# Turning round the second product of a fused attention and mixture kernel, and regrouping its 64-key products

## The chip, the cores and the metric

The kernel runs on one NeuronCore of a Trainium2 chip. The metric is the device time of one execution in microseconds. Its engines are TensorE (PE; PEld are its weight loads), VectorE (DVE), ScalarE (ACT), GpSimd (POOL) and SyncE (SP), which issues most of the DMAs. Each engine works through its own instructions in the order in which they were emitted; semaphores tie them together.

## The reference

For 8 batches of 12 heads, 448 tokens and 64 channels a head, attention with a sigmoid in place of the softmax; then a product with w_in, g = h - tanh(h), and a product with w_out. All in float32.

```python
scores = scale * np.matmul(q, k.transpose(0, 1, 3, 2)) - np.log(S)      # S = 448
attn = 1.0 / (1.0 + np.exp(-scores))
x = np.matmul(attn, v)             # (8, 12, 448, 64) -> (3584, 768)
h = x @ w_in                       # (768, 2048)
g = h - np.tanh(h)
out = g @ w_out                    # (2048, 768) -> (3584, 768)
```

## The kernel before

Float32 operands are split into two float16 parts (high and low), and a product is the sum of three float16 products. Two heads share the 128 partitions, so a batch has 6 pairs of heads (`NP`), numbered `g` over batches 1 to 7 in `stream` (`g % NP` is the place in the batch). Two neighbouring pairs, g and h = g + 1, make a step of `stream`.

A head has 448 keys: three tiles of 128 (`c` = 0, 1, 2) and a rest of 64 (`c == QT`). The rests of pair g and pair g + 1 are done together: `scores` (lines 384 to 401) then uses 64 rows by 64 columns of the array in four places, and `av` (lines 415 to 431), the product with v, does the same. For full tiles `scores` uses two blocks of 64 rows by 128 columns and `av` two blocks of 128 rows by 64 columns. Each instruction streams 448 columns. `units` (573) issues scores and the sigmoids (`weigh`, line 405, ACT); `keep` (584) splits them (`split_a`: line 411 on ACT, line 412 on DVE); `do_av` (558) issues the products with v of what is in `todo`; `close_acc` (549) evacuates an accumulator (`evac_x`, line 439, ACT) and calls `add_squares` (443 to 466).

`stream` is a generator; each `next` runs one block. A step of two pairs has the blocks B1 (scores c = 0, 1 of g; then the products with v of the pair h before, which closes it), B2 (scores c = 2 and the 64 keys of g and h), Sc (scales of the next two pairs, with a small PE product `pbn` in the PSUM bank "av"), B3 (scores c = 0, 1 of h; the products with v of g, the 64-key ones too, which closes g) and B4 (scores c = 2 of h, and the K and Q parts of the next odd pair, lines 369 to 372).

For the bound of a batch's tokens, `add_squares` sums the squares of its six x tiles: from batch 2 on, place 0 squares on ACT, places 1 to 4 square (line 456) and add (line 465) on POOL, place 4 (`NP - 2`) adds into `x2b`, and place 5 squares on ACT (line 454) into a tile of the tag "x2", which has two buffers. `token_norms` (687) then sums `x2b` and the last square by two PE matmuls (line 690, `nm`, in a buffer of the tag "sc", which has two and is shared with the scores), and DVE reduces `nm` (line 692), works out a scale and splits the six x tiles into `xhl` (lines 721 to 724).

A batch is then `moe1` (first product and the mixture; `product`, line 773) and `second`, which runs `moe2` (second product) and calls the blocks of the next batch's attention between its matmuls, at positions in `BLOCKS` (batch 1: `BLOCKS1`) counted in units of about 1 us of matmuls. From batch 2 on the positions are B4 at 8, B1 at 11, B2 at 16, Sc, B3 and B4 at 20, B1 at 27, B2 at 32, Sc, B3 and B4 at 36, B1 at 43, B2 at 48, Sc and B3 at 52. The B1 at 43 finishes the next batch's attention; `second` puts its `nm` three units behind it, at 46, and the other splits at 48 and 50. Batch 6 ends its blocks at 43; batch 7 has none. The rest of `mix` of the last g tile (`TAIL`) goes at 1 to 5.

`moe2` makes 128 tokens by 384 columns a matmul (line 857, `po`; stationary g, moving w_out), 288 to a batch, and for the 64 tokens that are left 96 matmuls of 64 columns of the array in pairs (line 905, `por`). Evacuation is on ACT (890) and DVE (894, 914).

Batch 0 and all preparation of the weights are laid out by hand in the string `ORDER`: each letter is a step (P one piece of the second product, B a block of `stream`, t and F the mixture's stages, A and a splits of w_out, C its conversion, X the scale of its second half, S and Z splits of w_in).

Of the kernel before, what the change touches and what calls it, by code (L numbers as in the profile page):

```python
# [8 lines left out]
F16 = mybir.dt.float16  # L9
# [24 lines left out]
class Builder:  # L34
# [7 lines left out]
        "vrrssvrsrrvvvvRrRrRRRMrRRRnRrRRGMRRwtMttRtRBtwRRtMwBgttMtRtRttMBttRtRttM"  # L42
        "tMBBtRttRMtBttMttMtRxtRtBRAtMtttAMtBttMttAttAttMMtAtPPtaRPRBPtBbtCaBCBAC"
        "PtFCCPBPCPPBZPPPCSBCPPBZCBCPPCCBPCCCSZBPPCCCPCXBaaAPaPPPBAPPaaaBBSPPSPSZ"
        "PSZSPPPPPPPSPBPPPZPPPNPZPSPZPSSNNPPSZPPZSSPPPPPPPPPPPP"
    )
# [244 lines left out]
    def w_out_scale(self, e):  # L291

        V = self.nc.vector
        self.w_out_bound(e)
        m = self.bound[e]
        total = self.sm.tile([P, 1], F32, name="wtot2")
        V.scalar_tensor_tensor(total, m, 1.05, m, op0=ALU.mult, op1=ALU.mult)
        S, inv = self.scale_of(total, f"swo{e}")
        self.Swo.append(S)
        V.tensor_copy(self.iSwo[:, e : e + 1], inv)  # L300
        h = slice(e * D, (e + 1) * D)
        V.tensor_copy(self.iSwo[h, 2:3], inv[h])

# [17 lines left out]
    def load_v(self, b, j, pool, tag, bufs):  # L321


        at = 0 if j % 2 == 0 else 2 * QT + 2
        n = 2 * QT + (0 if j % 2 else 2)
        t = pool.tile([P, n, D], F32, name="vn", tag=tag, bufs=bufs)
        self.nc.sync.dma_start(t, self.v[b, j // 2, :, at : at + n])
        return t
# [78 lines left out]

    def split_a(self, a):
        nc = self.nc
        A = self.tp.tile([P, 2, 2, self.S], F16, name="ahl", tag="t")  # L410
        nc.scalar.activation(A[:, 0], a[:, 0], AF.Copy, scale=A_SCALE)  # L411
        nc.vector.scalar_tensor_tensor(A[:, 1], a[:, 0], A_SCALE, A[:, 0], op0=ALU.mult, op1=ALU.subtract)  # L412
        return A

    def av(self, acc, v, A, c, odd):


        half = c == QT
        m = P // len(acc)
        prods = ((0, 0), (1, 0), (0, 1)) if A.dtype == F16 else ((0, 0),)  # L420
        for n, (w, x) in enumerate(prods):
            for i in range(len(acc)):
                for h in range(2):
# [4 lines left out]
                        A[k, x, h],  # L428
                        start=(n == 0 and (i == 1 if half else c == 0 and not odd)),
                        stop=(n == len(prods) - 1 and (i == 0 if half else c == QT - 1 and bool(odd))),  # L430
                    )
# [36 lines left out]
    def stream(self):  # L468
# [71 lines left out]
        yield 0, False  # L540
        todo = []

# [6 lines left out]
        def close_acc(g):  # L549
# [5 lines left out]
            for d in (sc, K, Q):  # L555
                d.pop(g)

        def do_av():
            for g, c, A in todo:
                odd = g % 2  # L560
                if c == QT:
                    open_acc(g + 1)
                    self.av([accs[g], accs[g + 1]], vv[g], A, c, odd)
                    close_acc(g)
                    continue
# [18 lines left out]
        def keep(g, cs, aa):  # L584
            if splits(g):
                aa = [self.split_a(a) for a in aa]
            todo.extend((g, c, a) for c, a in zip(cs, aa))

        for g in range(0, G, 2):
            h = g + 1  # L590
            early = g == 0

            aa = units(g, (0, 1))
            do_av()
            if early:
                prep_v(0)
                prep_v(1)
            keep(g, (0, 1), aa)
            load(g + 3)
# [3 lines left out]

            aa = units(g, (2, QT))
            if early:
                do_av()
            norms(g + 3)
            keep(g, (2, QT), aa)
            yield 2750, True
# [27 lines left out]
            yield 2750, True  # L637
        do_av()
        yield 1150, True

# [196 lines left out]
    def moe2(self, b, gs):  # L837
        nc = self.nc
        S = self.S
        ks = self.ks  # L840
        iK = self.sm.tile([P, 3], F32, name="iK")
        n = 1 if b == 0 else 3
        nc.vector.tensor_scalar(iK[:, :n], self.iSwo[:, :n], self.iSg, None, op0=ALU.mult)
        H = self.HALF
        base = b * S
        prods = ((0, 0), (0, 1), (1, 0))
        last = (self.NF - 1, 2)

        def store(o, j0, n, cols, queue=nc.sync):
            queue.dma_start(self.out[base + j0 : base + j0 + n, cols], o)  # L850

        nt = S // P

        def products(po, tk, f, e):
            for n, (x, w) in enumerate(prods):
                for i in e:
                    nc.tensor.matmul(  # L857
                        po[i][:, :H],
                        gs[f // 2][:, x, f % 2, tk * P : (tk + 1) * P],
                        self.wo[:, i * self.NF + 2 * ks[f // 2] + f % 2, w],  # L860
                        start=(f == 0 and n == 0),
                        stop=((f, n) == last),
                    )

        if b == 0:
            for e in range(2):
                for tk in range(nt):
                    po = {e: self.ps.tile([P, 512], F32, name="po", tag="mm", bufs=2)}
                    for f in range(0, self.NF, 2):
                        products(po, tk, f, (e,))  # L870
                        products(po, tk, f + 1, (e,))
                        if f + 2 == self.NF:
                            if (e, tk) == (1, 0):
                                nc.vector.tensor_scalar(iK[:, 1:], self.iSwo[:, 1:], self.iSg, None, op0=ALU.mult)
                            o = self.op.tile([P, H], F32, name="oh", tag="o", bufs=2)
                            nc.scalar.activation(o, po[e][:, :H], AF.Copy, scale=iK[:, e : e + 1])
                            store(o, tk * P, P, slice(e * H, (e + 1) * H))
                        yield 980
        else:
            for tk in range(nt):  # L880
                if b + 1 == self.B and tk % 2:
                    both = self.ps.tile([P, 2, 512], F32, name="po", tag="sc", bufs=2)
                    po = [both[:, e] for e in range(2)]
                else:
                    po = [self.ps.tile([P, 512], F32, name=f"po{e}", tag="mm", bufs=2) for e in range(2)]
                for f in range(self.NF):
                    products(po, tk, f, (0, 1))
                    if f == self.NF - 1:
                        o = self.op.tile([P, self.DM], F32, name="o", tag="o", bufs=2)
                        nc.scalar.activation(o[:, :H], po[0][:, :H], AF.Copy, scale=iK[:, 0:1])  # L890
                        if (b, tk) == (1, 0):
                            nc.scalar.activation(o[:, H:], po[1][:, :H], AF.Copy, scale=iK[:, 1:2])  # L892
                        else:
                            nc.vector.tensor_scalar(o[:, H:], po[1][:, :H], iK[:, 1:2], None, op0=ALU.mult)
                        store(o, tk * P, P, slice(0, self.DM))
                    yield 980
        nm = nt * P
        if b + 2 < self.B:
            po = self.ps.tile([P, 512], F32, name="por", tag="mm", bufs=2)
        else:  # L900
            po = self.ps.tile([P, 2, 512], F32, name="por", tag="sc", bufs=2)[:, 0]
        for f in range(self.NF):
            for n, (x, w) in enumerate(prods):
                for e in range(2):
                    nc.tensor.matmul(  # L905
                        po[e * D : (e + 1) * D, :H],
                        gs[f // 2][:, x, f % 2, nm:S],
                        self.wo[:, e * self.NF + 2 * ks[f // 2] + f % 2, w],
                        start=(f == 0 and n == 0),
                        stop=((f, n) == last),  # L910
                    )
            yield 560
        o = self.op.tile([P, H], F32, name="orem", tag="o", bufs=2)
        nc.vector.tensor_scalar(o, po[:, :H], iK[:, 2:3], None, op0=ALU.mult)  # L914
        for e in range(2):
            queue = nc.scalar if e and b + 1 == self.B else nc.sync
            store(o[e * D : (e + 1) * D], nm, S - nm, slice(e * H, (e + 1) * H), queue)


    def build(self):  # L920
# [13 lines left out]
        self.ihk0 = const("ihk0", KAPPA)  # L934
        self.iSwo = const("iswo", 1.0, 3)
        self.sums = [const(f"ss{i}", 0.0, 6) for i in range(2)]
# [147 lines left out]
    def second(self, b, blocks, alone, events):  # L1084
# [13 lines left out]
        events.sort(key=lambda e: e[0])  # L1098
        full = self.NF * (self.S // P)
        for k, _ in enumerate(self.moe2(b, self.gs)):  # L1100
            now = k + 1 if k < full else full + (k + 1 - full) / 2
            while events and events[0][0] <= now:
# [36 lines left out]
```

## Time and profile before

| what | us |
|---|---|
| runs | 1165.2, 1165.48, 1997.27; median 1165.48 |
| the profiled execution | 1166.29 |
| its span, first to last instruction | 1164.5 |
| PE busy | 1153.1 (99%) |
| DVE busy | 907.7 (78%) |
| ACT busy | 865.5 (74%) |
| POOL busy | 79.1 (7%) |

The profiled execution has 1.8 us around its span. Granted clock of TensorE 0.999. PE counts as busy from a matmul's start to its modelled end, and matmuls overlap, so the pace of PE is read from starts: a row of the timeline merges neighbouring instructions of one kind, and the start of the next row less its own start is what they took.

### The profile page before, as it was taken

The numbers are of one execution on the slowest core, as the hardware profiler recorded it, in microseconds if no ns is written. First come the engines' busy times: TensorE is split into PE (matmuls) and PEld (weight loads), VectorE is DVE, ScalarE is ACT, GpSimd is POOL, SyncE is SP. The second block draws the span as 40 slices with busy tenths as digits, with TensorE's granted clock in tenths as the row PEclk, the third lists the DMA queues.
The fourth block names the chain that finished last, engine by engine and source line by source line (L and its number), as shares of the span: only waits on it lengthen the run. The fifth ranks groups of instructions, "written<-read, shape, count | busy, mean of one in ns | idle before, by whom it ended". The sixth has DMA issues, their size and how long they took to land.

```text
span 1164.5 us, 18896 instructions
## 1 busy us (share of the span) xinstructions
PE 1153.1 (99%) x7563; PEld 597.4 (51%) x7564; DVE 907.7 (78%) x1308; ACT 865.5 (74%) x1195; POOL 79.1 (7%) x58
## 2 busy tenths in 40 slices
PE   9999999999999999999999999999999999999998
PEld 3345444555555555555555555555555555555565
DVE  6999999789777996679867897778976798646930
ACT  7988996588976888768887688867887688745820
POOL 0000000000120002200021000200022000300000
PEclk9999999999999999999999999999999999999999
DMA  9942171000222002210022101210012100000000
GB/s 358 357 163 64 42 224 53 29 7 1 80 75 64 7 1 78 62 53 1 17 76 62 40 1 31 82 58 24 1 55 84 53 1 9 23 28 7 1 14 35
DMA packets 34056, 70.43 MB, mean 60 GB/s; under 512 B 3888, under 2 KB 21040, under 8 KB 33968
## 3 DMA queue, kind: packets, MB, share of 16 engines
q1 hardware_dynamic: 33744, 68.89, 18.1%
q8 instruction: 59, 0.97, 0.4%
q10 hardware_dynamic: 224, 0.33, 0.1%
q14 instruction: 29, 0.24, 0.1%
HBM read 58.20 MB, written 11.01 MB: 59 GB/s over the span
## 4 chain that ended last, share of the span: by engine, by line
PE 73%; ACT 1%; issue 0%; DVE 0%; ACTq 0%
PE ph L773 28%; PE po L857 27%; PE sc L394 6%; PE acc L425 6%; PE por L905 5%; ACT a L405 0%; ACT ahl L411 0%; PE nm L690 0%; ACT sqn L335 0%; ACT x L439 0%; ACT Q L369 0%; DVE orem L914 0%; PE pbn L344 0%; ACT x L454 0%; ACT o L892 0%
## 5 line engine op out<-in xcount | busy, mean ns | idle before, releaser
L857 PE MATMUL po<-wo,g 128*128 128x384 f16 x2304 | 389.1, 326 | 3.1 <-DVE wo L240 1.6
L773 PE MATMUL ph<-xhl,wi 128*128 128x448 f16 x2016 | 382.6, 352 | 0.0
L857 PEld LDWEIGHTS <-g 128*128 128x128 f16 x2304 | 220.3, 98 | 170.1 <-issue 26.4
L773 PEld LDWEIGHTS <-wi 128*128 128x128 f16 x2016 | 196.7, 98 | 185.0 <-issue 2.1
L412 DVE SCALAR_TENSOR_TENSOR ahl<-a,ahl 128x896 f16<-128x896 f32 x126 | 162.7, 1326 | 125.6 <-ACT ahl L411 125.0
L405 ACT ACTIVATE a<-sc,nls,rn 128x896 f32<-128x896 f32 x147 | 155.8, 1090 | 37.4 <-PE sc L394 37.2
L811 ACT ACTIVATE u<-ph,ih 128x896 f32<-128x896 f32 x64 | 64.4, 1006 | 75.8 <-PE ph L773 74.0
L411 ACT ACTIVATE ahl<-a 128x896 f16<-128x896 f32 x126 | 113.2, 941 | 0.6
L394 PE MATMUL sc<-Q,K 64*128 64x448 f16 x1008 | 100.8, 353 | 0.9 <-DVE th L816 0.7
L815 DVE SCALAR_TENSOR_TENSOR m<-ph,ihk,u 128x896 f32<-128x896 f32 x64 | 73.5, 1149 | 25.6 <-ACT th L813 25.2
L766 ACT ACTIVATE g<-m,Sg 128x896 f16<-128x896 f32 x64 | 66.7, 1041 | 35.5 <-DVE m L829 28.5
L829 DVE COPY_PREDICATED m<-u,th 128x896 f32<-128x896 uint32 x64 | 77.2, 1206 | 6.8 <-ACT u L828 0.8
L425 PE MATMUL acc<-ahl,vhl 128*64 128x448 f16 (+1 forms) x864 | 80.6, 356 | 0.4 <-ACT tn L346 0.4
L456 POOL TENSOR_TENSOR x<-x 128x448 f32<-128x448 f32 x24 | 28.3, 1178 | 762.1 <-ACT x L439 762.1
L767 DVE SCALAR_TENSOR_TENSOR g<-m,Sg,g 128x896 f16<-128x896 f32 x64 | 73.4, 1147 | 6.8 <-ACT g L766 6.7
L826 DVE SCALAR_TENSOR_TENSOR m<-q,m 128x896 f32<-128x896 f32 x64 | 69.9, 1092 | 6.7 <-DVE m L822 0.5
L983 PE MATMUL ph<-x,wi 128*128 128x448 f32 x192 | 73.8, 540 | 0.0
L816 DVE SCALAR_TENSOR_TENSOR th<-ph,ih,th 128x896 f32<-128x896 f32 x64 | 73.3, 1145 | 0.0
L822 DVE SCALAR_TENSOR_TENSOR m<-q,m 128x896 f32<-128x896 f32 x64 | 69.6, 1087 | 0.0
L828 ACT ACTIVATE u<-u,b 128x896 f32<-128x896 f32 x64 | 66.7, 1042 | 1.9
L821 ACT ACTIVATE q<-u,b 128x896 f32<-128x896 f32 x64 | 65.8, 1028 | 0.0
L825 ACT ACTIVATE q<-u,b 128x896 f32<-128x896 f32 x64 | 65.8, 1028 | 0.0
(141 smaller groups left out, 1087.7 us busy)
## 6 DMA issues: line engine op xcount, KB each, us to landing
knn<-k SPq DMA_DIRECT2D x45, 224.0 KB, 2.6
qnn<-q SPq DMA_DIRECT2D x44, 224.0 KB, 2.6
rawo<-moe_w_out SPq DMA_DIRECT2D x22, 384.0 KB, 5.2
out<-o SPq DMA_DIRECT2D x21, 384.0 KB, 2.3
raw<-moe_w_in SPq DMA_DIRECT2D x13, 512.0 KB, 8.2
vn<-v SPq DMA_DIRECT2D x24, 256.0 KB, 2.8
wo<-moe_w_in SPq DMA_DIRECT2D x11, 512.0 KB, 8.3
vn<-v SPq DMA_DIRECT2D x24, 192.0 KB, 2.4
```

The source lines that it names most:

```text
L394: self.nc.tensor.matmul(ps[i * m : (i + 1) * m, h, : self.S], K[i][r, w, c * P : c * P + m], Q[i][r, x, :], start=(n == 0), stop=(n == len ...
L405: self.nc.scalar.activation(a[:, 0], ps[:, :, : self.S], AF.Sigmoid, bias=self.nls, scale=scale)
L411: nc.scalar.activation(A[:, 0], a[:, 0], AF.Copy, scale=A_SCALE)
L412: nc.vector.scalar_tensor_tensor(A[:, 1], a[:, 0], A_SCALE, A[:, 0], op0=ALU.mult, op1=ALU.subtract)
L425: self.nc.tensor.matmul(acc[i][h * D : (h + 1) * D, : self.S], v[k, w, 2 * QT + h if half else h * QT + c], A[k, x, h], start=(n == 0 and ...
L767: nc.vector.scalar_tensor_tensor(g[:, 1], m, Sg, g[:, 0], op0=ALU.mult, op1=ALU.subtract)
L773: self.nc.tensor.matmul(ph, self.wi[:, self.slot(c, k), part, e * P : (e + 1) * P], xhl[c][:, x, :], start=(i == 0), stop=(i == len(prods) ...
L815: V.scalar_tensor_tensor(m, ps, ihk, u, op0=ALU.mult, op1=ALU.mult)
L816: V.scalar_tensor_tensor(th, ps, ih, th, op0=ALU.mult, op1=ALU.subtract)
L829: V.copy_predicated(m, u.bitcast(U32), th)
L857: nc.tensor.matmul(po[i][:, :H], gs[f // 2][:, x, f % 2, tk * P : (tk + 1) * P], self.wo[:, i * self.NF + 2 * ks[f // 2] + f % 2, w], star ...
L983: nc.tensor.matmul(ph[:, e, :S], self.fp32(self.wi, self.slot(c, k))[:, 0, e * P : (e + 1) * P], xs[c], start=(c == 0), stop=(c == self.NC ...
```

## The change

- Second product: w_out's 128 columns become the stationary operand and all 448 tokens of g the moving one. A batch is 6 row blocks `d` of 48 matmuls 128*128 with 448 columns; the output is stored transposed (and turned back on the host). `por` is gone. From batch 1 on, the last two of block 0's 16 pieces are moved behind the eighth piece of block 1. The last block is evacuated and stored in two halves, on ACT and DVE. A batch has 96 yields, each counted as 7/12 of a unit; batch 0 has 48 P of six matmuls each in place of 64, and `ORDER` loses 16 P.
- Attention of batches 2 to 7: B1 is now scores c = 0 of g, products with v of the pair h before, the 64-key scores of g and h, and behind them the 64-key products with v of the two pairs before (`do_rest`), which closes both of them. B2 is scores c = 1, 2. B3 has no 64-key products and closes nothing. The split 64-key weights wait in a part of the w_out buffer; the 64-key part of v comes with the odd pair's load. Behind the last step `do_rest` runs once more.

```diff
@@ second product (moe2)
+        half = self.NC // 2
+        def products(po, d, f):
+            e, at = d // half, d % half * P
+            for n, (x, w) in enumerate(prods):
+                nc.tensor.matmul(
+                    po[:, :S],
+                    self.wo[:, e * self.NF + 2 * ks[f // 2] + f % 2, w, at : at + P],
+                    gs[f // 2][:, x, f % 2],
+                    start=(f == 0 and n == 0),
+                    stop=((f, n) == last),
+                )
+        def out(po, d):
...
+            if b + 1 == self.B and d == self.NC - 1:
+                h = S // 2
+                nc.scalar.activation(o[:, :h], po[:, :h], AF.Copy, scale=iv)
+                nc.scalar.dma_start(self.out[rows, b * S : b * S + h], o[:, :h])
+                nc.vector.tensor_scalar(o[:, h:], po[:, h:S], iv, None, op0=ALU.mult)
+                nc.sync.dma_start(self.out[rows, b * S + h : (b + 1) * S], o[:, h:])
+                return
+            if b == 0 or d % 2 or (b, d) == (1, 0):
+                nc.scalar.activation(o, po[:, :S], AF.Copy, scale=iv)
+            else:
+                nc.vector.tensor_scalar(o, po[:, :S], iv, None, op0=ALU.mult)
+            nc.sync.dma_start(self.out[rows, cols], o)
+        held = 2
+        order = [(d, f) for d in range(self.NC) for f in range(self.NF)]
+        if b:
+            late = [order.pop(self.NF - held) for _ in range(held)]
+            at = self.NF - held + self.NF // 2
+            order[at:at] = late
+        for d, f in order:
+            if f == 0:
+                po[d] = self.ps.tile([P, 512], F32, name="po", tag="mm", bufs=2)
+            products(po[d], d, f)
...
+            if b or f % 2:
+                yield 567
@@ stream
+        def do_rest():
+            while kept:
+                g, A = kept.pop()
+                self.av([accs[g], accs[g + 1]], vv[g + 1], A, QT, 0, True)
+                close_acc(g)
+                close_acc(g + 1)
         def do_av():
             for g, c, A in todo:
                 odd = g % 2
+                if splits(g):
+                    if c == 0:
+                        open_acc(g)
+                    self.av([accs[g]], vv[g], A, c, odd, True)
+                    continue
...
-            aa = units(g, (0, 1))
-            do_av()
+            first, second = ((0, QT), (1, 2)) if splits(g) else ((0, 1), (2, QT))
+            if splits(g):
+                aa = units(g, (0,))
+                do_av()
+                aa += units(g, (QT,))
+                do_rest()
...
-            aa = units(g, (2, QT))
+            aa = units(g, second)
...
         do_av()
+        do_rest()
@@ second
-            now = k + 1 if k < full else full + (k + 1 - full) / 2
+            now = (k + 1) * 7 / 12
```

## Rows read from the trace of the kernel before

**Rows 1.** The page: busy time of the engines, the granted clock in 40 slices, and the chain of work that ended last, by engine.
```profile
PE 1153.1 (99%) x7563; PEld 597.4 (51%) x7564; DVE 907.7 (78%) x1308; ACT 865.5 (74%) x1195; POOL 79.1 (7%) x58
...
PEclk9999999999999999999999999999999999999999
...
PE 73%; ACT 1%; issue 0%; DVE 0%; ACTq 0%
```
**Rows 2.** Whom PE waited for in the whole span: us in total, times, longest us.
```profile
PE po L857 <- DVE wo L240: 1.6, 3, 0.6
...
PE sc L394 <- DVE th L816: 0.7, 1, 0.7
PE po L857 <- DVE g L767: 0.7, 1, 0.7
...
PE po L857 <- ACT g L766: 0.4, 1, 0.4
```
**Rows 3.** Timeline of PE at the end of batch 6 and in batch 7, where no block of attention stands between: start us, us, engine, line, operation, count.
```profile
1043.10 7.99 PE L905 MATMUL por<-wo,g 128*64 128x384 f16 x96
1051.02 54.66 PE L773 MATMUL ph<-xhl,wi 128*128 128x448 f16 x288
1105.51 46.96 PE L857 MATMUL po<-wo,g 128*128 128x384 f16 x288
1152.41 7.99 PE L905 MATMUL por<-wo,g 128*64 128x384 f16 x96
```
**Rows 4.** Timeline of PE in batch 2's second product, around the B1 at 43 and the B2 at 48.
```profile
486.50 1.31 PE L394 MATMUL sc<-Q,K 64*128 64x448 f16 x12
...
487.74 1.89 PE L425 MATMUL acc<-ahl,vhl 128*64 128x448 f16 x18
...
489.56 3.10 PE L857 MATMUL po<-wo,g 128*128 128x384 f16 x18
...
492.50 0.35 PE L690 MATMUL nm<-x2b,onesb 128*128 128x448 bf16 x1
...
492.69 0.35 PE L690 MATMUL nm<-x,onesb 128*128 128x448 bf16 x1
...
494.92 1.43 PE L394 MATMUL sc<-Q,K 64*128 64x448 f16 x18
...
496.28 1.98 PE L905 MATMUL por<-wo,g 128*64 128x384 f16 x22
```
**Rows 5.** Timeline of ACT and DVE in the same stretch; in brackets the idle time before and what ended it.
```profile
487.28 2.09 ACT L405 ACTIVATE a<-sc,nls,rn 128x896 f32<-128x896 f32 x2 [2.33 <-PE sc L394]
...
489.67 0.64 ACT L439 ACTIVATE x<-acc,rn 128x448 f32<-128x448 f32 x1 [0.30 <-PE acc L425]
...
490.40 0.58 ACT L454 ACTIVATE x<-x 128x448 bf16<-128x448 f32 x1
490.88 1.77 ACT L411 ACTIVATE ahl<-a 128x896 f16<-128x896 f32 x2
491.85 2.09 DVE L412 SCALAR_TENSOR_TENSOR ahl<-a,ahl 128x896 f16<-128x896 f32 x2 [4.04 <-ACT ahl L411]
...
493.86 0.62 DVE L692 TENSOR_REDUCE m<-nm 128x1 f32<-128x448 f32 x1
```
**Rows 6.** The squares of place 4 in the B3 at 36 of the same batch, on ACT and POOL; then the instructions of line 456 in the whole span (shortest, median and longest ns).
```profile
479.00 0.63 ACT L439 ACTIVATE x<-acc,rn 128x448 f32<-128x448 f32 x1
...
479.77 1.46 POOL L456 TENSOR_TENSOR x<-x 128x448 f32<-128x448 f32 x1 [11.23 <-ACT x L439]
...
481.31 1.87 POOL L465 TENSOR_TENSOR x2b<-x,x 128x448 bf16<-128x448 f32 x1
...
L456 POOL TENSOR_TENSOR x<-x x24: 933/936/1486, 305.5 to 1029.2; 128x448 f32<-128x448 f32 x24
```
**Rows 7.** Timeline of PE in batch 0's second product, where it waits.
```profile
146.61 1.15 PE L857 MATMUL po<-wo,g 128*128 128x384 f16 x6
148.21 0.50 PE L857 MATMUL po<-wo,g 128*128 128x384 f16 x2 [0.44 <-ACT g L766]
149.39 1.80 PE L857 MATMUL po<-wo,g 128*128 128x384 f16 x10 [0.69 <-DVE g L767]
...
182.69 0.32 PE L857 MATMUL po<-wo,g 128*128 128x384 f16 x1
183.51 1.14 PE L857 MATMUL po<-wo,g 128*128 128x384 f16 x6 [0.49 <-DVE wo L240]
185.22 0.97 PE L857 MATMUL po<-wo,g 128*128 128x384 f16 x5 [0.57 <-DVE wo L240]
...
191.64 5.50 PE L857 MATMUL po<-wo,g 128*128 128x384 f16 x31
197.71 2.60 PE L857 MATMUL po<-wo,g 128*128 128x384 f16 x15 [0.57 <-DVE wo L240]
```
**Rows 8.** Timeline of batch 2's B1 at 11: its first scores, and the DVE work of the B4 before it that is still going on.
```profile
436.93 1.31 PE L394 MATMUL sc<-Q,K 64*128 64x448 f16 x12
...
437.65 1.08 DVE L412 SCALAR_TENSOR_TENSOR ahl<-a,ahl 128x896 f16<-128x896 f32 x1
...
438.65 0.68 DVE L372 SCALAR_TENSOR_TENSOR Q<-qnn,sn,Q 128x448 f16<-128x448 f32 x1
```
**Rows 9.** Timeline of the end of the span: the last evacuation.
```profile
1160.44 0.62 DVE L914 TENSOR_SCALAR orem<-por,iK 128x384 f32<-128x384 f32 x1 [7.31 <-PE por L905]
```

More of the change, by code (lines that the diff above doesn't have):

```diff
@@ L42 @@
         "vrrssvrsrrvvvvRrRrRRRMrRRRnRrRRGMRRwtMttRtRBtwRRtMwBgttMtRtRttMBttRtRttM"
-        "tMBBtRttRMtBttMttMtRxtRtBRAtMtttAMtBttMttAttAttMMtAtPPtaRPRBPtBbtCaBCBAC"
-        "PtFCCPBPCPPBZPPPCSBCPPBZCBCPPCCBPCCCSZBPPCCCPCXBaaAPaPPPBAPPaaaBBSPPSPSZ"
-        "PSZSPPPPPPPSPBPPPZPPPNPZPSPZPSSNNPPSZPPZSSPPPPPPPPPPPP"
+        "tMBBtRttRMtBttMttMtRxtRtBRAtMtttAMtBttMttAttAttMMtAtPPtaRRBPtBbtCaBCBACP"
+        "tFCCPBPCPPBZPPCSBCPPBZCBCPPCCBPCCCSZBPCCCPCXBaaAPaPPPBAPaaaBBSPPSPSZPSZS"
+        "PPPPPPSPBPPZPPPNPZPSPZSSNNPPSZPZSSPPPP"
     )
@@ L300, in w_out_scale @@
         V.tensor_copy(self.iSwo[:, e : e + 1], inv)
-        h = slice(e * D, (e + 1) * D)
-        V.tensor_copy(self.iSwo[h, 2:3], inv[h])
     def split_w_out(self, e):
@@ L321, in load_v @@
     def load_v(self, b, j, pool, tag, bufs):
-        at = 0 if j % 2 == 0 else 2 * QT + 2
-        n = 2 * QT + (0 if j % 2 else 2)
+        first = 2 * QT + (2 if b < self.AV32 else 0)
+        at = j % 2 * first
+        n = 4 * QT + 2 - first if j % 2 else first
         t = pool.tile([P, n, D], F32, name="vn", tag=tag, bufs=bufs)
@@ L406, in weigh, with split_a @@
         return a
-    def split_a(self, a):
+    def split_a(self, a, kept):
         nc = self.nc
-        A = self.tp.tile([P, 2, 2, self.S], F16, name="ahl", tag="t")
+        if kept:
+            A = self.scratch((self.NF - self.SHIFT_O) * 2 * self.HALF, 4 * self.S).rearrange("p (x h n) -> p x h n", x=2, h=2)
+        else:
+            A = self.tp.tile([P, 2, 2, self.S], F16, name="ahl", tag="t")
         nc.scalar.activation(A[:, 0], a[:, 0], AF.Copy, scale=A_SCALE)
@@ L413, in split_a, with av @@
         return A
-    def av(self, acc, v, A, c, odd):
+    def av(self, acc, v, A, c, odd, late=False):
         half = c == QT
+        if late:
+            begin, end = (not half and c == 0,) * 2, (half,) * 2
+        else:
+            begin = (False, True) if half else (c == 0 and not odd,)
+            end = (True, False) if half else (c == QT - 1 and bool(odd),)
         m = P // len(acc)
@@ L428, in av @@
                         A[k, x, h],
-                        start=(n == 0 and (i == 1 if half else c == 0 and not odd)),
-                        stop=(n == len(prods) - 1 and (i == 0 if half else c == QT - 1 and bool(odd))),
+                        start=(n == 0 and begin[i]),
+                        stop=(n == len(prods) - 1 and end[i]),
                     )
@@ L540, in stream @@
         yield 0, False
-        todo = []
+        todo, kept = [], []
         def open_acc(g):
@@ L585, in keep @@
             if splits(g):
-                aa = [self.split_a(a) for a in aa]
-            todo.extend((g, c, a) for c, a in zip(cs, aa))
+                aa = [self.split_a(a, c == QT) for c, a in zip(cs, aa)]
+            for c, a in zip(cs, aa):
+                if splits(g) and c == QT:
+                    kept.append((g, a))
+                else:
+                    todo.append((g, c, a))
         for g in range(0, G, 2):
@@ L591, in stream @@
             early = g == 0
-            aa = units(g, (0, 1))
-            do_av()
+            first, second = ((0, QT), (1, 2)) if splits(g) else ((0, 1), (2, QT))
[4 more added lines that the diff above has]
+                do_rest()
+            else:
+                aa = units(g, first)
+                do_av()
             if early:
@@ L597, in stream @@
                 prep_v(1)
-            keep(g, (0, 1), aa)
+            keep(g, first, aa)
             load(g + 3)
@@ L607, in stream @@
             norms(g + 3)
-            keep(g, (2, QT), aa)
+            keep(g, second, aa)
             yield 2750, True
@@ L840, in moe2 @@
         ks = self.ks
-        iK = self.sm.tile([P, 3], F32, name="iK")
-        n = 1 if b == 0 else 3
+        iK = self.sm.tile([P, 2], F32, name="iK")
+        n = 1 if b == 0 else 2
         nc.vector.tensor_scalar(iK[:, :n], self.iSwo[:, :n], self.iSg, None, op0=ALU.mult)
         H = self.HALF
-        base = b * S
+        cols = slice(b * S, (b + 1) * S)
         prods = ((0, 0), (0, 1), (1, 0))
         last = (self.NF - 1, 2)
-        def store(o, j0, n, cols, queue=nc.sync):
-            queue.dma_start(self.out[base + j0 : base + j0 + n, cols], o)
@@ L852, in moe2 @@
-        nt = S // P
-        def products(po, tk, f, e):
+        half = self.NC // 2
+        def products(po, d, f):
+            e, at = d // half, d % half * P
             for n, (x, w) in enumerate(prods):
[L856 to L917, printed above, removed]
+                nc.tensor.matmul(
[5 more added lines that the diff above has]
+                )
@@ new lines, in out @@
+        def out(po, d):
+            iv = iK[:, d // half : d // half + 1]
+            rows = slice(d * P, (d + 1) * P)
+            o = self.op.tile([P, S], F32, name="o", tag="o", bufs=2)
+            if b + 1 == self.B and d == self.NC - 1:
[7 more added lines that the diff above has]
+                nc.scalar.activation(o, po[:, :S], AF.Copy, scale=iv)
+            else:
+                nc.vector.tensor_scalar(o, po[:, :S], iv, None, op0=ALU.mult)
+            nc.sync.dma_start(self.out[rows, cols], o)
@@ new lines, in moe2 @@
+        held = 2
[4 more added lines that the diff above has]
+            order[at:at] = late
+        po = {}
+        for d, f in order:
+            if f == 0:
+                po[d] = self.ps.tile([P, 512], F32, name="po", tag="mm", bufs=2)
+            products(po[d], d, f)
+            if f == self.NF - 1:
+                if (b, d) == (0, half):
+                    nc.vector.tensor_scalar(iK[:, 1:], self.iSwo[:, 1:], self.iSg, None, op0=ALU.mult)
+                out(po.pop(d), d)
+            if b or f % 2:
+                yield 567
@@ L934, in build @@
         self.ihk0 = const("ihk0", KAPPA)
-        self.iSwo = const("iswo", 1.0, 3)
+        self.iSwo = const("iswo", 1.0, 2)
         self.sums = [const(f"ss{i}", 0.0, 6) for i in range(2)]
@@ L1098, in second @@
         events.sort(key=lambda e: e[0])
-        full = self.NF * (self.S // P)
         for k, _ in enumerate(self.moe2(b, self.gs)):
-            now = k + 1 if k < full else full + (k + 1 - full) / 2
+            now = (k + 1) * 7 / 12
             while events and events[0][0] <= now:
@@ L1122 @@
     rest = v[:, :, QT * P :].reshape(B, H // 4, 2, 2, D, D).transpose(0, 1, 2, 4, 3, 5).reshape(B, H // 4, P, 2, D)
+    n = Builder.AV32
+    v_first = np.concatenate([heads[:n, :, :, 0], rest[:n], heads[:n, :, :, 1]], axis=3)
+    v_later = np.concatenate([heads[n:, :, :, 0], heads[n:, :, :, 1], rest[n:]], axis=3)
     arrays = {
@@ L1125 @@
         "k": pairs(k),
-        "v": np.ascontiguousarray(np.concatenate([heads[:, :, :, 0], rest, heads[:, :, :, 1]], axis=3)),
+        "v": np.concatenate([v_first, v_later]),
         "moe_w_in": np.ascontiguousarray(moe_w_in).view(np.uint64),
@@ L1132 @@
     }
-    shape = (B * S, H * D)
+    shape = (H * D, B * S)
     args["out"] = nc.dram_tensor("out", shape, F32, kind="ExternalOutput").ap()
@@ L1137 @@
     r = run_bass_kernel_spmd(nc, [arrays], core_ids=[0])
-    return r.results[0]["out"]
+    return np.ascontiguousarray(r.results[0]["out"].T)
```

## The prediction

> **What bounds the kernel now.** I read the page first: PE is busy 99% of the span, the chain that ended last lies on PE, and the granted clock is at its upper level, 2.4 GHz, in all 40 slices [rows 1]. Since a matmul's end is modelled, that does not yet say that PE never stands still, so I read whom PE waited for: a handful of waits, none over 1 us, on the splits of w_out, the first g tiles and the mixture [rows 2]. By the timeline those lie in batch 0 [rows 7] and early in batch 1. From batch 2 on PE waits for nothing. So three things count: the pace of PE's own stream, a PE wait that goes, and a PE wait that comes. Work of ACT, DVE, POOL and the queues counts only where PE comes to wait for it.
>
> **Part 1, the second product.** Before, a batch takes 46.90 us for 288 matmuls of 384 columns (from 1105.51 to 1152.41) and 7.92 us for the 96 of `por` (from 1043.10 to 1051.02) [rows 3], 54.82 us with the change into and out of the 64-column form. The new form, 128*128 with 448 columns, is in the trace as the first product: 288 from 1051.02 to 1105.51, 54.49 us, 0.1892 each [rows 3]. The new second product is also 288 of these. It saves 0.33 us a batch, 2.6 us in eight, less 0.1 for the exit that the last batch doesn't have: 2.5 us. Why so little: the streamed columns are the same (288 x 384 + 48 x 384 = 288 x 448). 46.8/288 = 0.1625 us for 384 columns and 0.1892 for 448 make 0.417 ns a column and 2.5 ns beside; 48 instructions' places fewer a batch give 0.12 us, and the two changes of form the rest. Bounds: 1 us (the changes cost nothing) to 3.5 us.
>
> The Trainium skill, TensorEngine Tiling, section Instruction Overhead, puts some 60 cycles on each matmul, an estimated 25 ns at 2.4 GHz. By that, 384 places fewer would give 9.6 us in place of 1.0 and the forecast would be 8.6 us lower, 1163.5. The two rows of 384 and 448 columns leave room for 2.5 ns, so I don't take it.
>
> There is still one weight load of 128 columns a matmul, under a longer matmul. Evacuations are six of 448 columns where there were seven of 384, half each on ACT and DVE, and a block now has the other PSUM buffer to go on in: off PE's path. The stores move the same bytes, and the v loads only shift 64 KB from one pair's load to the next; no PE wait on a DMA stands in the rows [rows 2].
>
> **Part 2, the order of the attention blocks.** PE pays when the shape of its blocks changes. Six pairs of scores at 0.189 are 1.13 us, and they take 1.24 (486.50 to 487.74); nine pairs with v are 1.70 and take 1.82; three pairs of scores and three groups of four, 1.13, take 1.36 with two changes [rows 4]. So a change costs 0.10 us. Before, a step of two pairs makes 3 in B1 (in, to the products with v, out), 3 in B2, 5 in Sc to B4: 11. After: B1 has 4 (in, v, 64-key, out; the 64-key scores and products share a form), B2 2, Sc to B4 4: 10. One less in 17 of the 18 steps: 1.7 us. No row shows 64-key products straight behind 64-key scores; if that costs a change too, the gain is 0. I take 1.7, since groups of four of one line run without a gap.
>
> B1 now needs more, sooner. Its products with v begin after one unit of scores, 0.57 us earlier, and the 64-key scores need the odd pair's Q, made in the B4 before. At the B1 at 11 that B4 has just ended: DVE ends the last split at 438.73 and the low part of Q at 439.33, with B1 begun at 436.93 [rows 8]. After, the low half of the third tile is wanted at 1.81 + 0.38 us into B1 (439.1) and that of Q at 2.49 + 0.19 (439.6). It holds by 0.3 us; price if not, 0 to 0.5 us in six batches.
>
> **Part 3, batch 0.** The pieces P are now 1.134 us long and 48. In the old rows PE loses 0.62 us before 148.21, 0.85 before 149.39, 0.66 before 183.51, 0.74 in the row at 183.51, and 1.03 in the row at 191.64 (31 matmuls are 5.04 us, the next row starts 6.07 later) [rows 7]. The last three wait for the splits of w_out's second half. The step X stands at the same time in P work (19.3 us against 19.5), but piece 24, the first to need it, comes after 27.2 us and not 23.4: 2.4 us of waiting goes. The wait for the last g goes nearly whole, 1.3 of 1.47, since two longer pieces and not one stand ahead of it behind the B before. Against it: one P less ahead of the first B1, which already waits 0.7 us for the mixture [rows 2], costs 0.7; and piece 16 now follows piece 15 with no block between, while one of the two PSUM buffers collects the sums of w_out, so PE waits for an evacuation, some 0.5. Net 2.5 us gained; bounds 4.5 gained to 2 lost. Batch 1 I put at 0.
>
> **Part 4, the end of each batch's attention.** Here a new wait comes. Before, place 4 of a batch closes in the B3 at 36; in that one, ACT's x ends at 479.63, POOL squares (1.46 us) and adds (1.87) until 483.18 [rows 6], and `nm` reads the sum at 492.50 [rows 4], 9 us later. After, places 4 and 5 both close at the end of the B1 at 43, and `nm` is still three units behind it, which is now 5 yields, 15 matmuls, 2.84 us. From the start of that B1:
> - PE: scores 0.67 with the change, products with v 1.82 (2.49), 64-key scores 0.57 (3.06), 64-key products 0.67 (3.73), 15 matmuls (6.57): PE stands at `nm`.
> - ACT: the first sigmoid starts 0.78 behind its scores' start [rows 4, 5], so the second, behind the 64-key scores, starts at 3.27 and ends at 4.3; x of place 4 follows, 0.64, until 4.94.
> - POOL starts 0.14 later, squares for 0.94 (the median of line 456; 0.93 to 1.49) and adds for 1.87 [rows 6]: 7.97. The first `nm` is 1.4 us late.
> - ACT's square of place 5 wants one of the two x2 buffers, and both are read by that last POOL add. It starts at 8.05 and ends at 8.63 (0.58 [rows 5]). The second `nm`, due at 6.76, comes at 8.65: PE has lost 1.9 us.
> - Behind that square on ACT stand the two splits, and behind them on DVE the reduction of `nm`. From the first split's start to the second DVE split's end it was 3.06 us (490.88 to 493.94 [rows 5]); from 8.55 that is 11.6, and the reduction (0.62) ends at 12.2. `nm` holds one of the two score buffers. PE is at B2 at 8.84 + 12 x 0.189 = 11.1 and wants that buffer for the second unit at 11.7: 0.5 us more.
>
> Together 2.4 us in each of batches 1 to 5. In batch 6 the last step has no scores ahead of the closing: x ends at 3.35, the square at 7.0, `nm` was due at 5.6: 1.5. Sum 13.5 us. Nothing hides it, since PE is the bound and its order is fixed. Later, the last x split comes about 5.7 us behind B3's start as before, and the next first product starts 6.4 behind it (7.8 before), so I count no third wait. Bounds: 1 us a batch (a quicker POOL, no second wait), 6 us; 3.3 us a batch (squares of 1.49, a longer second wait), 20.
>
> The squares of line 456 run from 0.93 to 1.49 us [rows 6]; with the long ones throughout the forecast would be 3 us higher. The Trainium skill, GPSIMD Engine Reference, section Specifications, says that POOL shares its SBUF interfaces with VectorE. By that, the short one is the likelier, since DVE stands idle there until ACT's splits come; the trace has the long one, 1.46, beside DVE work.
>
> **Part 5, the end.** The last evacuation is 0.62 us [rows 9]; two halves of 224 columns side by side save about 0.2.
>
> **The sum.** 1166.29 - 2.5 - 1.7 - 2.5 + 13.5 - 0.2 = 1172.9 for the profiled execution, which lies 0.8 above the median of the runs (1165.48); so 1172.1.
>
> **Rivals.** (A) The wait of part 4 doesn't come, or is hidden: only parts 1, 2, 3 and 5 count, 1158.6. For it: POOL is busy 7% [rows 1], and the chain was never waited for. Against it: the chain's durations alone, 0.64 + 0.94 + 1.87 behind a sigmoid, exceed the 2.84 us that cover it. (B) On the slower side, the held ACT queue: the square that waits for POOL holds ACT from 5.5 to 8.05, 2.5 us, and with it splits, norms, sigmoids and evacuations. If ACT or DVE has not caught up by the next first product, PE pays that once more, 2.5 us in five batches: 1184.6. The place is the last `xhl` against the first `ph`; it decides where the last x split ends over 2.8 us behind `ph`'s start, when PE reaches the sixth x. For it: DVE is busy 78% and the mixture that follows loads ACT and DVE nearly as much as PE; against it the 1.4 us that stay by my count. (C) The regrouping saves no change: 1.7 us higher, within the first case.
>
> **How the numbers follow.** The wait as worked out, 1172.1: 0.72; its own range, by the bounds of parts 2 to 4, 1166 to 1178. A: 0.13. B: 0.15. The range takes in A whole and the first case, 1158 to 1179, and leaves out most of B. 2% of the time is 23 us, about what a measurement of this kernel can tell from no change; no case reaches it, and I leave 0.03 for slower (B with more) and 0.02 for faster.
>
> **What would show it.** Right: PE waits under `nm` (line numbers aside) for ACT's square or POOL's add, some 1.5 to 2 us, six times from batch 1 on; ACT's last square of a batch ends a wait for POOL; a second short PE wait in the B2 behind it; 288 matmuls of `po` in 54.5 us where no block stands; no PE wait for w_out's second half. Wrong: no PE wait at `nm` (A); waits at the start of `ph` (B); 64-key products 0.1 us behind their scores (C).

## The result, and the profile after

The changed kernel takes 1172.01 us (median; 1170.4 to 1174.35), the kernel before 1166.24 in the same count of runs: a ratio of 1.0053, 95% interval 1.0043 to 1.0063. The forecast was 1172.1. It is slower by half a per cent, well inside 2%. The profiled execution took 1171.91 us, its span is 1170.1 (before 1164.5). The total is as forecast; the terms are not, as shown below.

The page after, in the lines of [rows 1]:
```profile
PE 1151.4 (98%) x6795; PEld 557.2 (48%) x6796; DVE 888.2 (76%) x1299; ACT 865.5 (74%) x1195; POOL 68.1 (6%) x58
...
PEclk9999999999999999999999999999999999999999
...
PE 89%; ACT 5%; DVE 3%; issue 2%; POOL 1%; POOLq 0%; DVEq 0%; ACTq 0%
```
PE is the bound still, but the chain that ended last now leaves PE for ACT, DVE and POOL. (Its shares don't compare with [rows 1]: there the chain was followed over 74% of the span only, here over all of it.) Whom PE waited for (us in total, times, longest), to set beside [rows 2]:
```profile
PE po L883 <- ACT o L903: 3.6, 1, 3.6
PE nm L720 <- POOL x2b L471: 2.5, 5, 0.5
PE pbn L343 <- ACT sqn L334: 2.3, 3, 1.0
PE nm L720 <- ACT x L460: 1.5, 6, 0.3
PE sc L393 <- DVE th L846: 1.2, 1, 1.2
...
PE acc L431 <- ACT tn L345: 1.2, 2, 1.0
PE sc L393 <- DVE m L722: 1.0, 5, 0.2
```
The waits for `wo` and for g of before are gone. Two kinds came: at `nm` and behind it, five or six times, and one long wait for an evacuation. These sums are short of what PE loses, since a wait counts only from the modelled end of the matmul before; starts tell it better. The B1 at 43 of batch 2 on PE, to set beside [rows 4]:
```profile
488.64 0.74 PE L393 MATMUL sc<-Q,K 64*128 64x448 f16 x6
489.31 1.89 PE L431 MATMUL acc<-ahl,vhl 128*64 128x448 f16 x18
491.13 0.76 PE L393 MATMUL sc<-Q,K 64*64 64x448 f16 x12
491.73 0.74 PE L431 MATMUL acc<-wo,vhl 64*64 64x448 f16 x12
492.40 3.01 PE L883 MATMUL po<-g,wo 128*128 128x448 f16 x15
495.91 0.35 PE L720 MATMUL nm<-x2b,onesb 128*128 128x448 bf16 x1 [0.50 <-POOL x2b L471]
496.52 0.35 PE L720 MATMUL nm<-x,onesb 128*128 128x448 bf16 x1 [0.26 <-ACT x L460]
496.70 2.43 PE L883 MATMUL po<-g,wo 128*128 128x448 f16 x12
499.07 0.74 PE L393 MATMUL sc<-Q,K 64*128 64x448 f16 x6
500.02 0.74 PE L393 MATMUL sc<-Q,K 64*128 64x448 f16 x6 [0.21 <-DVE m L722]
```
And ACT, POOL and DVE in that stretch, to set beside [rows 5, 6]:
```profile
491.95 1.10 ACT L404 ACTIVATE a<-sc,nls,rn 128x896 f32<-128x896 f32 x1 [1.43 <-PE sc L393]
492.95 1.15 ACT L445 ACTIVATE x<-acc,rn 128x448 f32<-128x448 f32 x2
493.72 0.93 POOL L462 TENSOR_TENSOR x<-x 128x448 f32<-128x448 f32 x1 [18.56 <-ACT x L445]
494.73 1.13 POOL L471 TENSOR_TENSOR x2b<-x,x 128x448 bf16<-128x448 f32 x1
495.89 0.58 ACT L460 ACTIVATE x<-x 128x448 bf16<-128x448 f32 x1 [1.79 <-POOL x2b L471]
...
499.35 0.62 DVE L722 TENSOR_REDUCE m<-nm 128x1 f32<-128x448 f32 x1
```
The reader is to see, from the top: the second sigmoid starts 3.31 us into the block, POOL's sum is there at 495.86, and ACT stood 1.79 us before its square, whose buffer POOL's add still read (third_x2_buffer, below, tests that). The first `nm` starts 0.67 us late (492.40 + 2.84 is 495.24), the second another 0.42, and the second unit of B2's scores, which needs `nm`'s buffer, 0.37 (0.95 behind the first, where 0.58 is usual). That is 1.46 us a batch, five times; batch 6 has 0.65. Together 7.9 us.

The second product of batch 7 keeps the pace of the first product ahead of it, row beside row, as [rows 3] had it for the first product alone:
```profile
1057.01 54.64 PE L803 MATMUL ph<-xhl,wi 128*128 128x448 f16 x288
1111.49 54.64 PE L883 MATMUL po<-g,wo 128*128 128x448 f16 x288
```
Batch 0, in place of [rows 7], on PE and then on ACT:
```profile
159.00 0.16 PE L343 MATMUL pbn<-ss,onesb 128*128 128x4 bf16 x1 [0.96 <-ACT sqn L334]
...
172.81 1.31 PE L883 MATMUL po<-g,wo 128*128 128x448 f16 x6
173.95 0.68 PE L201 MATMUL wl<-stb,onesb 128*128 128x384 bf16 x3
178.25 1.56 PE L883 MATMUL po<-g,wo 128*128 128x448 f16 x6 [3.62 <-ACT o L903]
```
```profile
172.79 0.70 ACT L237 ACTIVATE wi<-wi,swi_s 128x512 f16<-128x512 f32 x1
173.41 2.06 ACT L404 ACTIVATE a<-sc,nls,rn 128x896 f32<-128x896 f32 x2
...
177.59 0.62 ACT L903 ACTIVATE o<-po,iK 128x448 f32<-128x448 f32 x1
```
Piece 15 ends near 174.1, and its evacuation starts at 177.59: ACT has no gap between, it is working off the block that stood ahead of piece 15 (sigmoids whose first scores were issued at 169.16, an x, its square, two norms). Piece 16 needs that PSUM buffer. By starts PE loses 3.8 us there. While PE stood its granted clock stayed at 1.00; 0.9 us after PE had gone on, at 179.1, it fell to 0.50, that is 1.2 GHz, until 182.5. The stretches (PE, PEld, DVE, ACT, POOL busy, granted clock, DMA):
```profile
178.00:179.50 1.50, 1.25 (x6) 0.63 (x6) 0.98 (x2) 0.20 (x1) 0.00 (x0) 0.88 0.27 103
179.50:182.50 3.00, 3.00 (x20) 0.66 (x18) 2.12 (x9) 1.09 (x1) 0.00 (x0) 0.50 0.07 25
```
The row at 180.07 shows the price: 18 matmuls of scores from 180.07 to 182.56, 2.49 us, where such a B2 takes 1.36 [rows 4]. From the start of piece 16 to the end of that block it is 4.31 us, and in piece15_earlier (below), at the full clock, 2.76 (175.63 to 178.39): the low clock cost 1.5 us. The wait at 159.00 is a third loss: 0.96 us, where `pbn` waited 0.38 before.

By stages, from the first matmul of each batch's first product in the traces (us):

| stretch | before | after | turned_alone (below) |
|---|---|---|---|
| until batch 1's first product | 226.3 | 227.4 | 226.3 |
| batch 1 | 144.6 | 145.8 | 143.8 |
| batches 2 to 5, each | 137.4 | 138.1 | 137.0 |
| batch 6 | 130.8 | 131.5 | 130.4 |
| batch 7 to the span's end | 113.4 | 113.1 | 113.1 |

Each of batches 2 to 6 loses 0.7 us; batch 0, 1.1; batch 1, 1.2; only the last, which has no attention beside it, is faster. Two things are mixed into these rows. The regrouping moves twelve 64-key products with v, three groups of 0.19 or 0.57 us, from the stretch of batch 1 (48 before, 36 after) to that of batch 6 (24 before, 36 after). And the low clock of batch 0 isn't in every execution: of the six of the changed kernel the two with a mean granted clock of 1.0 took 1170.4 and 1170.81 us, the four with 0.997 to 0.999 took 1171.91 and more, and the traced one of turned_alone has no such stretch.

### The profile page after: what moved, and what is told of

It is laid out like the page before. It is cut to its first block, busy times and chain, and to the rows that moved or that the text cites. A ratio compares the mean times of both kernels' runs of the same rounds, so it can differ in the third digit from the quotient of the medians.

```text
span 1170.1 us, 17354 instructions
## 1 busy us (share of the span) xinstructions
PE 1151.4 (98%) x6795; PEld 557.2 (48%) x6796; DVE 888.2 (76%) x1299; ACT 865.5 (74%) x1195; POOL 68.1 (6%) x58
## 4 chain that ended last, share of the span: by engine, by line
PE 89%; ACT 5%; DVE 3%; issue 2%; POOL 1%; POOLq 0%; DVEq 0%; ACTq 0%
PE po L883 33%; PE ph L803 32%; PE sc L393 8%; PE acc L431 8%; PE ph L990 6%; ACT a L404 1%; ACT ahl L413 1%; DVE stb L181 1%; PE cs L207 1%; PE warm L97 1%; POOL x2b L471 0%; POOL x L462 0%; ACT sqn L334 0%; DVE wo L414 0%; ACT x L445 0%
## 5 line engine op out<-in xcount | busy, mean ns | idle before, releaser
L883 PE MATMUL po<-g,wo 128*128 128x448 f16 x2304 | 451.2, 353 | 3.6 <-ACT o L903 3.6
L883 PEld LDWEIGHTS <-wo 128*128 128x128 f16 x2304 | 219.6, 98 | 231.4 <-issue 34.9
L414 DVE SCALAR_TENSOR_TENSOR ahl<-a,ahl 128x896 f16<-128x896 f32 x108 | 119.6, 1135 | 148.5 <-ACT ahl L413 148.5
L393 PE MATMUL sc<-Q,K 64*128 64x448 f16 (+1 forms) x1008 | 104.1, 357 | 2.3 <-DVE th L846 1.2
L413 ACT ACTIVATE ahl<-a 128x896 f16<-128x896 f32 x108 | 98.1, 941 | 0.6
L431 PE MATMUL acc<-ahl,vhl 128*64 128x448 f16 x648 | 68.2, 355 | 1.2 <-ACT tn L345 1.2
```

Source lines behind the costliest of these rows:

```text
L393: self.nc.tensor.matmul(ps[i * m : (i + 1) * m, h, : self.S], K[i][r, w, c * P : c * P + m], Q[i][r, x, :], start=(n == 0), stop=(n == len ...
L431: self.nc.tensor.matmul(acc[i][h * D : (h + 1) * D, : self.S], v[k, w, 2 * QT + h if half else h * QT + c], A[k, x, h], start=(n == 0 and ...
L883: nc.tensor.matmul(po[:, :S], self.wo[:, e * self.NF + 2 * ks[f // 2] + f % 2, w, at : at + P], gs[f // 2][:, x, f % 2], start=(f == 0 and ...
```

## The experiments

The theory after the result: the time went to two places, the chain behind the last closing of a batch (7.9 us), and piece 16 of batch 0 (3.8 us and some 1.5 at the low clock); the rest of the change gains a few us. Rivals: the turned product itself costs; ACT's queue is the bound and not POOL's chain; waits taken away only move.

**turned_alone**: the second product turned, the attention's order as before.
```diff
+        regroup = lambda g: False
...
-            first, second = ((0, QT), (1, 2)) if splits(g) else ((0, 1), (2, QT))
+            first, second = ((0, QT), (1, 2)) if regroup(g) else ((0, 1), (2, QT))
...
-        first = 2 * QT + (2 if b < self.AV32 else 0)
+        first = 2 * QT + 2
...
```


> The changed kernel with its attention in the order of before (64-key products with v in B3, v's rest with the even pair). If the wait at the batch's bound comes from the regrouped attention, as predicted, PE waits for nothing at nm and the time is that of before less the second product's pace (2.5 us) and tail (0.2) plus what batch 0 lost in the changed kernel's trace (some 1.6 to 2.7 us more waiting than before): about 1165, at most 1167. If the turned product itself costs (its evacuations, its stores, its held pieces), the time stays at 1170 or more and PE waits in batches 2 to 7.

1164.8 us (1163.35 to 1166.79), ratio to before 0.999, interval 0.9981 to 0.9999; PE waits for nothing from batch 2 on. So the turned product alone is a small gain, although it has the wait of piece 16 too (3.1 us in its trace). The regrouping adds 7.2 us to it (1172.01 less 1164.8), 1.1 in each of batches 2 to 5: its 1.46 of waits less 0.3 for three changes of shape.

**regrouped_alone**: the kernel before with `stream`, `av`, `split_a` and the v layout of the changed one.

> The kernel before with the changed attention order alone. By my theory the wait at nm (1.1 us) and at the second unit of B2's scores (0.4 us) is there six and five times, 8 us, less one change of the array's shape in 17 steps, 1.7 us: 1172 to 1173, slower than before by 0.5%. If the wait needs the turned product too (its counting of positions), the time is 1164.5 to 1166.

1178.66 us (1178.22 to 1179.77), ratio 1.0107, interval 1.0093 to 1.0121. The direction held; the size, 12.4 us, is double. Its PE waits hold the expected ones and others:
```profile
PE po L889 <- DVE o L926: 2.9, 11, 0.6
PE sc L395 <- DVE m L724: 2.6, 5, 0.5
...
PE nm L722 <- POOL x2b L473: 2.1, 5, 0.4
PE nm L722 <- ACT x L462: 1.6, 6, 0.3
```
The old second product fills two PSUM buffers at once and wants both back for the next 128 tokens. Behind the regrouped B1 its evacuations come late on ACT, and DVE's behind them, and PE stands there twice a batch, by starts 6.6 us in all:
```profile
449.48 0.34 PE L889 MATMUL po<-wo,g 128*128 128x384 f16 x1
450.12 3.90 PE L889 MATMUL po<-wo,g 128*128 128x384 f16 x23 [0.30 <-DVE o L926]
```
That is one matmul, then 0.64 us to the start of the next in place of 0.16. The wait in B2 is longer too: 0.69 us by starts, where the changed kernel has 0.37. So the two parts are not independent: the turned product's blocks, which use one buffer and leave the other to evacuate, hide some 5 us that the regrouping costs by itself (1178.66 less 1166.27, 12.4, against 7.2 on the turned product).

**square4_on_act**: place 4 squares on ACT, POOL adds up to place 3 only, `nm` is three matmuls.
```diff
+        tail = pool and j >= self.NP - 2
+        x2 = self.xp.tile([P, self.S], BF16 if last or tail else F32, name="x2", tag="x2", bufs=2)
+        if last or tail or j == 0 or not pool:
...
+        elif tail:
+            self.x2b = (*(self.x2b if last else (self.x2,)), x2)
...
```


> The changed kernel with place 4's square on ACT instead of POOL and summed by a third nm matmul, so that neither POOL operation stands between the last closing and nm and ACT's last square waits for no POOL add. By my theory the wait at nm falls from 1.1 to under 0.2 us and the one in B2 from 0.37 to under 0.3: 5.5 to 7 us less than the changed kernel, 1165 to 1166.5. If ACT's queue by itself is the bound there (its sigmoid, two x and now two squares), the waits stay and the time is 1171 to 1173.

1166.13 us (1165.3 to 1167.97), 5.9 less than the changed kernel; ratio to before 1.0, interval 0.9992 to 1.0009. The three `nm` follow closely, 0.57 us to the next `po`, and the first of them is 2.85 us behind the block's end (490.62), with 15 matmuls between:
```profile
493.47 0.35 PE L723 MATMUL nm<-x2b,onesb 128*128 128x448 bf16 x1
493.66 0.54 PE L723 MATMUL nm<-x,onesb 128*128 128x448 bf16 x2
494.04 2.43 PE L886 MATMUL po<-g,wo 128*128 128x448 f16 x12
```
That settles that the new wait of each batch is this chain, and that it is worth what the starts said: 7.9 less six third matmuls, 1.1, less 0.16 that stays in each of five B2, 0.8, is 6.0.

**third_x2_buffer**: which half of the chain is dear, POOL's sum or the held ACT queue.
```diff
-        x2 = self.xp.tile([P, self.S], BF16 if last else F32, name="x2", tag="x2", bufs=2)
+        x2 = self.xp.tile([P, self.S], BF16 if last else F32, name="x2", tag="x2", bufs=3)
...
```
The other line of the edit gives the same third buffer to a step of batch 0 that shares the tag.

> The changed kernel with a third buffer for the squares, so that ACT's last square no longer waits for POOL's add. By my theory nm still waits for POOL, longer than the 0.67 us of now since DVE's splits come beside the add (1.13 us now, up to 1.87 as before the change), while the 0.4 us behind it on ACT's square and the 0.37 us in B2 go: 1171 to 1174, no gain. The rival, that the held ACT queue is the cost: 4 to 5 us less, 1167 to 1168.

1167.49 us (1166.49 to 1168.77): 4.5 less than the changed kernel. The rival was right. ACT's square no longer waits and everything behind it comes two microseconds sooner; POOL's add takes its 1.13 us still, with DVE's first split beside it only for the last 0.15:
```profile
493.72 0.58 ACT L460 ACTIVATE x<-x 128x448 bf16<-128x448 f32 x1
494.19 1.13 POOL L471 TENSOR_TENSOR x2b<-x,x 128x448 bf16<-128x448 f32 x1
...
495.37 0.35 PE L720 MATMUL nm<-x2b,onesb 128*128 128x448 bf16 x1 [0.43 <-POOL x2b L471]
```
The second `nm` follows at 495.56. What stays is 0.6 us before the first. So of the 7.9 us the larger part, 0.42 at the second `nm` and 0.37 in B2 of the 1.46 a batch, came through the one shared buffer.

**piece15_earlier**: one P of `ORDER` moved ahead of a block and two splits of w_in (a part of one line of the string).
```diff
...
-CCCSZBPCCCPCX
+CCCPSZBCCCPCX
...
```


> The changed kernel with piece 15 of batch 0's second product moved ahead of the block that stood before it, so that its evacuation lies ahead of that block's work on ACT and piece 16 doesn't follow it at once. By my theory the wait of 3.8 us there and the 1.3 us that PE then loses at a granted clock of 0.5 both go: 5 us less than the changed kernel, 1167, and the granted clock there stays at 1. The rival: the wait only moves, to the next thing that wants the PSUM buffer or to the splits of w_out's second half: 1170 or more.

1169.16 us (1168.73 to 1170.49), 2.9 less. The 3.6 us wait and the low clock are gone, but part of it came back 12 us later, where a score unit waits for a sigmoid on an ACT that is itself behind:
```profile
160.17 0.16 PE L343 MATMUL pbn<-ss,onesb 128*128 128x4 bf16 x1 [1.42 <-ACT sqn L334]
...
190.34 0.74 PE L393 MATMUL sc<-Q,K 64*128 64x448 f16 x6 [1.23 <-ACT a L404]
```
Between theory and rival, then. In the traces 5.3 us went (3.8 and 1.5), and batch 1's first product starts 2.6 us sooner. Of the 2.7 between, 1.6 returned behind the moved piece: 1.3 by starts at 190.34 and 0.3 at 185.72. The other 1.2 stand ahead of it already at 160.17, where the changed kernel has 159.00: the batch began later in this execution, and `pbn` waited 1.42 us and not 0.96. So they are not the work of the edit.

**no_held_pieces**: `held = 0`, so block 0 is done in one run.

> The changed kernel with held = 0: the last two pieces of block 0 stay in their place. In the changed kernel's trace batch 2's second product starts at 427.65 and the last g tile is there at 438.96; piece 14 would come at 436.4. So PE should wait 2.2 to 2.6 us in seven batches: 1187 to 1190. The rival, that the holding is worth nothing since the last g tile is early enough: 1172.

1188.92 us (1188.5 to 1189.49), ratio 1.0196, interval 1.0182 to 1.021: the time is as expected. The wait came in six batches and not in seven: the stretches of batches 2 to 6 are 2.2 us longer than the changed kernel's, that of batch 7 4.3, with a stretch of low clock behind its wait, and that of batch 1 is 0.5 shorter. In batch 7:
```profile
1123.67 8.11 PE L883 MATMUL po<-g,wo 128*128 128x448 f16 x42
1133.79 0.54 PE L883 MATMUL po<-g,wo 128*128 128x448 f16 x2 [2.01 <-ACT g L796]
1134.98 7.33 PE L883 MATMUL po<-g,wo 128*128 128x448 f16 x29 [0.65 <-DVE g L797]
```
After 14 pieces, 42 matmuls, the last g is not there. The turned product comes to the last g after 14 of 16 pieces of one block, 7.9 us, and needs the held pieces to be no worse than before.

**both_mended**: square4_on_act and piece15_earlier together.

> The changed kernel with place 4's square on ACT and with piece 15 earlier. The two waits lie in different stages, so by my theory their gains add: 1172.0 less 5.9 (the one alone) less 2.9 (the other alone), 1163.3, faster than before (1166.3) by 0.25%. If they share a cause, it stays at 1165 to 1166.

1163.45 us (1162.95 to 1164.58), ratio 0.998, interval 0.997 to 0.9989. The gains add.

**turned_alone_piece15**: the turned product, the old order of attention, piece 15 earlier.

> The turned product with the attention order of before, and with piece 15 earlier. If the wait in batch 0 is the only thing that the turned product adds, this is turned_alone (1164.8) less 2.9: 1161.9, the fastest of all, and PE waits for nothing over 0.3 us from batch 2 on. The rival: what remains of the regrouping is worth its 1.7 us, and both_mended is the faster one.

1161.71 us (1161.1 to 1161.86), ratio 0.9961, interval 0.9947 to 0.9975: the fastest. Against it both_mended is still 1.7 us slower. Batches 2 to 5 take 137.0 us each in both (the third `nm`, 0.19, and 0.16 in B2 eat the three changes of shape). Batch 1 is 0.9 us longer and batch 6 0.6, and that 0.6 is the twelve products that the regrouping moves there from batch 1. So the loss arises in batch 1, which has two waits, 0.6 us before `pbn` and 1.0 behind it, that are 0 and 0.15 with the old order. So even mended the regrouping doesn't pay here.

## Why the prediction was right, and where by luck

- **The second product's pace** (2.5 us): as worked out; 288 matmuls in 54.5 us, the same as the first product's. turned_alone bears it out: 137.0 us a batch where it was 137.4, a gain of 0.4 for 0.33.
- **The changes of shape** (1.7 us): the B1 takes 3.76 us (488.64 to 492.40) against 3.73 forecast. The open question is answered: the 64-key products start 0.60 us behind their scores' first, three groups at 0.19 are 0.57, so there is no change between the two, and rival C falls. The gain has been timed only together with other terms.
- **The new wait at the end of each batch** (13.5 us): the mechanism was right in each link, POOL's sum, the square held by its buffer, the reduction, the score buffer. The size was not: 7.9 us. The mis-sized term is POOL's add, put at 1.87 us by [rows 6]; it took 1.13 in all six, with nothing of DVE beside it. So 0.74 less at `nm`, where PE loses 1.09 us and not the 1.9 of the forecast, and less behind it. third_x2_buffer shows that the shared buffer, not the sum, was its greater half.
- **Batch 0** (2.5 us gained): this step failed. The waits for w_out's second half and most of that for the last g went, as said. But "PE waits for an evacuation, some 0.5" was 3.8 us, for I had counted PE's work between pieces 15 and 16 and not ACT's queue in front of the evacuation; and 1.5 us at the low clock came with it in the traced execution. The wait at `pbn`, 0.6 us longer than before, isn't in the prediction either. The stretch is 1.1 us longer instead of 2.8 shorter (2.5 and the pace). piece15_earlier gives 2.9 of it back.
- **Batch 1** (0 beside the other terms): two waits for ACT behind the fuller B1, 0.6 us before `pbn` and 1.0 for the accumulator behind it, where turned_alone has 0.15. It is 1.2 us longer than before, though twelve products, 0.57 us, left it; the other terms alone make it 0.8.
- **The end** (0.2): the two halves don't run side by side; ACT's took from 1166.22 to 1166.67 and DVE's started at 1166.70. With the pace, batch 7 is 0.3 us shorter.
- **The sum**: 5.6 us too much in one term, about 4 too little in batch 0 and batch 1, and 0.6 in batch 6, which got the twelve products. For the profiled execution I had 1172.9, and it took 1171.91. That the median fits to 0.1 us is chance; that the wait of part 4 made the kernel slower is not.
- **The rivals**: A is refuted by the waits; B, a third wait at the next first product, didn't come: nothing of it stands among PE's waits. That the held ACT queue is where the time goes, B's ground, was nearer to the truth than I gave it.

## What to carry to other kernels

When several results are closed at one point, list the chain from there to the next reader on the bounding engine, with the buffers that it shares: a ring of two buffers between a slow engine and a queue in order holds all that the queue carries, and one more buffer gave the larger part of that back here (4.5 us of 7.9). For an evacuation on PE's path, count the work in the evacuating engine's queue at the point where it is emitted, not the bounding engine's work until it is needed. A layout that fills one PSUM buffer at a time forgives late evacuations (it hid some 5 us here, the difference of what the regrouping cost in the two layouts: 12.4 and 7.2); one that fills both at once doesn't.

## What the hardware showed

POOL's add of two 128x448 tiles took 1.13 or 1.14 us in all seven closings of the changed kernel, where it took 1.87 beside a DVE split before [rows 6]. The lines of `x2b` over the whole span, after:
```profile
L471 POOL TENSOR_TENSOR x2b<-x,x x7: 1127/1130/1140, 194.3 to 1045.4; 128x448 bf16<-128x448 f32 x7
```
In six of the seven no DVE instruction ran beside it. In the first, at 194.3, a DVE split of w_out ran beside it from its start; the add kept its 1.14 us and the split took 1.96, where its neighbours take 1.02. So DVE work beside it doesn't always lengthen an add. In batch 2 of the changed kernel, in order of time:
```profile
470.35 1.13 POOL L471 TENSOR_TENSOR x<-x,x 128x448 f32<-128x448 f32 x1
470.58 1.84 DVE L414 SCALAR_TENSOR_TENSOR ahl<-a,ahl 128x896 f16<-128x896 f32 x1 [5.95 <-ACT ahl L413]
471.56 1.67 POOL L462 TENSOR_TENSOR x<-x 128x448 f32<-128x448 f32 x1
```
With nothing beside them the split takes 1.09 us and the square 0.93. Here the one that starts while the other is under way is the longer one, on either engine. That fits [rows 6] too, whose add started 0.8 us into a DVE split. The Trainium skill, GPSIMD Engine Reference, section Specifications, has POOL share its SBUF interfaces with VectorE; the traces agree, and put the price at 0.7 to 0.9 us for the later of the two.

The granted clock fell to 0.50 (1.2 GHz) for about 3 us after PE had stood 3.6 us in the changed kernel, 3.0 us in third_x2_buffer and 3.3 us in no_held_pieces; after 3.1 us in turned_alone and in square4_on_act it stayed at 1.00. In no_held_pieces it fell in batch 7 too, after waits of 2.0 and 0.65 us with two matmuls between, and stayed at 1.00 in batches 2 to 6 after 1.4 and 0.65 us with two between. So waits of one length may or may not cost it.
